# First key quarter turned by TensorE, one MLP copy on VectorE, later side work on ScalarE

## The chip, the cores and the metric

The kernel runs on one core of one Trainium2 chip. The metric is the device time of one launch in microseconds (us), as a median over runs. Five engines work side by side, each through its own list of instructions in order: TensorE (PE, matmuls; PEld is its weight load), VectorE (DVE), ScalarE (ACT), GpSimd (POOL) and SyncE (SP, which mostly issues DMAs). DMA queues move data between HBM and the on-chip SBUF. Matmuls write to PSUM, from which DVE and ACT read.

## The reference

The input x has 2048 tokens of 512 values. After a LayerNorm, two branches start from the same xn:

```python
xn = _layernorm(x, axis=-1)
s = attention(xn, k_cache, v_cache, wq, wo)   # 32 heads of 128, 2048 keys, all softmaxed
h = gelu(layernorm(xn) @ w1)                  # 512 -> 512
hs = shift_by_quarters(h) @ w2                # token shifts +1, -1, +2, -2
x1 = xn + hs
g = silu(x1 + gelu(layernorm(x1) @ w3) @ w4)  # 512 -> 1792 -> 512
return x + s * g
```

All tensors are bf16; the keys and values are given per head as 2048 x 128.

## The kernel before, in words

The attention is cut into 128 **units**: 8 groups of 4 heads, 4 blocks of 512 queries in each group, 4 heads in each block. A unit has 8 **slots** (`n` counts slots over all units, `p` is the slot in the unit). In each slot PE makes two 128x512 score matmuls (`ps_s<-qT,kT`), ACT takes the exponential of both (`s_slot`, L222), and PE multiplies an older slot's result with V (`ps_o<-pT,vb`, `pv_slot`), 4 to 12 slots behind. There are two score buffers in PSUM and two buffers for `ps_o`. DVE adds the exponentials of a unit (`add_first` L228, `add_next` L233), folds the sum (`fold`, L237 and L238), and at the end multiplies `ps_o` with the reciprocal sum (`norm`, L305), which frees the `ps_o` buffer. For the first four and the last two units the row sums are made by PE (`sums`, `ps_sum<-ones_t,acc`); for all others the folded sum is turned by a DMA and reduced by DVE (`turned(u)` says which).

The order is written out by hand: one loop over `n` emits, for each slot, the score matmuls, the V matmuls, then the side work of that slot. Side work is the Q projection, the Wo products (`wo_todo` holds those that are due, as pairs of slots 4 and 5) and the MLP. The MLP is a queue of chunks, some matmuls of which are taken in slots 2, 3, 6 and 7. Stage 1 (w1) has 16 chunks, one for each tile of 128 tokens; its results carry a scale per token. The result of a chunk in `ps_m` is copied to `pre` (L591) by ACT. Two chunks make a pair, and a gelu follows: `square` (ACT, L550) twice, `poly` (DVE, L554), `tanh` (ACT, L559) twice, `last` (DVE, L562).

Which slot ACT's squares and tanhs get is decided by a running **debt**. Each slot adds `EXP_OVER` (0.2) and subtracts the side matmuls that PE had in it; each side operation of ACT adds `SMALL` (2.4). A waiting operation in `act_late` goes out when the debt plus its own cost is covered by the side matmuls that `ahead` sees in the next two slots. `at(n, fn)` puts a function off to slot `n`, `soft(n)` moves it to slot 3, 5 or 7.

The start, before the loop: x tiles are loaded (SP and ACT queues), weights by POOL's queue, and the keys of head 0 in four quarters by transposing DMAs on SP (L173; `KSPLIT` is 4). Meanwhile PE runs 48 small matmuls on the identity (`warm_up`, L125). `first_stats` (L418) makes the LayerNorm of the first four tiles; tile 0 is normalised by ACT (L442). `first_tokens` turns the four tiles by matmuls with the identity, copies them to `xnT` (L492, L490), makes the first queries, copies them to `qT` (L505, L503), and takes the first scores in four groups of quarter and half (`s_half`, exponential L513). The first group reads key quarter 0, the second quarter 1.

All matmuls have the line L125, that of the helper `mm`. A helper `pin` keeps each instruction in the order in which it is written.

Of the kernel before, what the change touches and what calls it, by code (L numbers as in the profile page):

```python
# [8 lines left out]
ACT = mybir.ActivationFunctionType  # L9
# [8 lines left out]
def kernel(  # L18
# [15 lines left out]
    nc = tc.nc  # L34
# [133 lines left out]
    def load_k(h, pieces):  # L168
        w = Sk // KSPLIT
        for i in pieces:  # L170
            if i == 0:
                kTs[h] = kp.tile([P, Sk], BF16, name="kT")
            pin(nc.sync.dma_start(  # L173
                out=kTs[h][:, i * w:(i + 1) * w],
                in_=A_k_cache[0, h, i * w:(i + 1) * w, :], transpose=True))

    def load_v(h, halves, eng=nc.sync):
        v = A_v_cache[0, h].rearrange("(i p j) d -> p i j d", p=P, j=KJ)
# [86 lines left out]
    def turned(u):  # L265
        return T0 <= u < T1
# [148 lines left out]
        pin(nc.vector.bn_aggr(out=mv1[t][:], in_=bn[:]))  # L415
        rsqrt(rs1[t][:], mv1[t][:, 1:2])

    def first_stats():  # L418
        junk = gtp.tile([P, D], BF16, tag="pre", name="pre")
        pin(nc.scalar.activation(  # L420
            out=junk[:], in_=ln[3][:], func=ACT.Identity, scale=1.0 / D, accum_out=mvA[:, 3, 0:1]))
        pin(nc.scalar.activation(
            out=junk[:], in_=ln[3][:], func=ACT.Square, scale=-1.0, bias=mvA[:, 3, 0:1],
            accum_out=mvA[:, 3, 1:2]))
        xn0 = ph1.tile([P, D], BF16, tag="xn", bufs=5, name="xn")
        nb = smp.tile([P, 1], FP32, tag="nm", name="nb")

        def power(t):
            pin(nc.gpsimd.tensor_tensor(
                out=rsA[:, t:t + 1], in0=mvA[:, t, 1:2], in1=nhalf[:, 0:1], op=ALU.pow))  # L430

        for t in range(3):
            pin(nc.vector.bn_stats(out=bnA[:, t, 0:2, :], in_=ln[t][:]))
            pin(nc.vector.bn_aggr(out=mvA[:, t, :], in_=bnA[:, t, :, :]))
            power(t)
            if t == 1:
                pin(nc.vector.tensor_scalar(
                    out=nb[:], in0=mvA[:, 0, 0:1], scalar1=rsA[:, 0:1], scalar2=-1.0, op0=ALU.mult, op1=ALU.mult))
                pin(nc.vector.tensor_scalar(
                    out=mvA[:, 3, 1:2], in0=mvA[:, 3, 1:2], scalar1=1.0 / D, scalar2=EPS, op0=ALU.mult, op1=ALU.add))  # L440
                power(3)
        pin(nc.scalar.activation(  # L442
            out=xn0[:], in_=ln.pop(0)[:], func=ACT.Identity, scale=rsA[:, 0:1], bias=nb[:]))
        xn1 = ln1_norm(1)
        xn3 = ln1_norm(3)
        return xn0, xn1, ln1_norm(2), xn3
# [6 lines left out]
    def ln1_norm(t):  # L453
        xin = ln.pop(t)
        xn = ph1.tile([P, D], BF16, tag="xn", bufs=5, name="xn")
        norm1(t, xn[:], xin[:])
        return xn
# [9 lines left out]
    def warm_up(n):  # L467
        wt = psS.tile([P, 2, 512], FP32, name="ps_s")
        for _ in range(n):
            mm(wt[:, 0, 0:P], ident[:], ident[:], True, True)  # L470
# [111 lines left out]
    def gelu_chunk(lhs, rhs, j, scale, dest):  # L582
        def run(i, n):
            if i == 0:
                mlp["ps"] = psX.tile([P, 512], FP32, tag="xm", name="ps_m")
            mm(mlp["ps"][:], lhs(i), rhs(i), i == 0, i == DC - 1)
            if i == DC - 1:
                if j == 0:
                    mlp["pre"] = gtp.tile([P, 2, 512], BF16, name="pre")
                pre = mlp["pre"]  # L590
                pin(nc.scalar.activation(out=pre[:, j, :], in_=mlp["ps"][:], func=ACT.Identity,  # L591
                                         **({} if scale is None else dict(scale=scale))))
                debt[0] += SMALL
                if j == 1:
                    gelu_pair(pre, dest(), n)
        run.size = DC
        return run
# [200 lines left out]
    pin(nc.scalar.activation(out=act1[:], in_=nhalf[:, 0:1], func=ACT.Identity))  # L798
    for h in range(HG - 1):
        load_w(h, nc.gpsimd)  # L800
    load_k(0, range(KSPLIT))
    load_v(0, (0, 1))
    for i in range(2):
        load_k(1, (2 * i, 2 * i + 1))
        load_v(1, (i,))
    warm_up(WARM)
    xns_0 = first_stats()
    load_w(HG - 1, nc.gpsimd)
    for t in range(4, 6):
        ln1_load(t, nc.gpsimd)  # L810
# [52 lines left out]
    def normed(u):  # L863
        norm(u)
        gg, qq, hh = units[u]
        if hh == HG - 1 and (gg, qq) in deferred:
            at((u + 4) * SPU + 4, lambda: pin(nc.sync.dma_start(out=o_d[(gg, qq)][:], in_=oTs[(gg, qq)][:])))
        elif hh == HG - 1:
            wo_todo.extend((gg, 4 * qq + ts) for ts in range(4))
            if gg == NG - 1:  # L870
                fin_load(4 * qq)

    for n in range(NS):
# [24 lines left out]
            turned_sums(u - 2)  # L898
        if p == 0 and u >= 1:
            add_next(u - 1, 3)  # L900
            if not turned(u - 1):
                fold(u - 1)
        if p == (1 if mlp.get("stage") == 2 or u >= QUIET else 2) and HG < u < NU - 2:
            q_copy(u + 2)
# [3 lines left out]
            acc_turn(u - 1)  # L908
        if p == 1 and u > LATE:
            normed(u - 3)  # L910
        if p == (3 if u >= LATE else 2) and u >= 2 and turned(u - 2):
            bcast(u - 2)
        if n in norms:
# [44 lines left out]
            fn()  # L958
        x = mm_count[0] - mm_before - 4
        debt[0] = max(0.0, debt[0] + EXP_OVER - x) if n >= HALF else 0.0  # L960
        if act_late and debt[0] + SMALL <= ahead(n + 1) + ahead(n + 2):
            act_late.popleft()(n)
            debt[0] += SMALL
        if p == SPU - 1 and u >= 2 and turned(u - 2) and (u < LATE or u == NU - 1):
# [96 lines left out]
```

## Time and profile before

| What | us |
|---|---|
| Median of three runs | 1247.88 |
| Lowest and highest run | 1246.97, 1249.35 |
| The profiled execution | 1246.4 |
| Its span, first to last instruction | 1244.6 |
| PE busy | 1232.4 |
| ACT busy | 1129.0 |
| DVE busy | 1116.5 |
| ACT exponentials (L222), 1020 of them | 1017.7 |
| Span up to the first matmul on keys | 9.01 |

The profile gives for every engine its busy time and, by groups of instructions, the idle time ahead of them and what ended it. Matmuls overlap in the array, so one can last longer than the distance from its start to the next one's. A row of the timeline has the start, the time to the end of the last of the merged instructions, the engine, the line, what is written and read, and in brackets the idle time before it and what ended it. The granted TensorE clock is at full speed in nearly every slice of the span.

### The profile page before, as it was taken

Reading aid. Unit: us, or ns where it says so; the run is one execution under the profiler, and the core shown is the slowest. Engines: PE = TensorE matmul, PEld = TensorE weight load, DVE = VectorE, ACT = ScalarE, POOL = GpSimd, SP = SyncE. Lnnn points to the kernel's source line nnn. Section 1 sums busy time; section 2 is a strip of 40 time slices with the busy share of each in tenths; the row PEclk is TensorE's granted clock in tenths of the full one; section 3 lists DMA queues with packets and bytes.
Section 4 is the critical chain, followed back from the end, with each engine's and each line's share of the span. In section 5 each row is a group of like instructions: output and inputs, shape, how many; then the busy total and the mean of one; then the engine's idle time right before and its main releaser. Section 6 shows DMA issues by size and latency. Waiting matters only on the chain.

```text
span 1244.6 us, 16527 instructions
## 1 busy us (share of the span) xinstructions
PE 1232.4 (99%) x5702; PEld 597.3 (48%) x5816; DVE 1116.5 (90%) x1520; ACT 1129.0 (91%) x1285; POOL 172.2 (14%) x299
## 2 busy tenths in 40 slices
PE   9999999999999999999999999999999999999998
PEld 5444444444444444444444444444444444444444
DVE  7999999999899988899988889999888999888998
ACT  8999998888999888899998889998888999998992
POOL 5563003432111000000100000010000000000110
PEclk9999999999999999999999999999999999999999
DMA  9665573665634455234474235734446233563563
GB/s 202 124 118 101 101 141 77 129 126 123 145 65 112 100 102 120 55 89 75 109 148 90 68 77 111 132 76 82 86 101 124 56 89 65 127 140 76 105 149 108
DMA packets 248788, 131.42 MB, mean 106 GB/s; under 512 B 200000, under 2 KB 225472, under 8 KB 248704
## 3 DMA queue, kind: packets, MB, share of 16 engines
q1 hardware_dynamic: 239296, 104.46, 40.8%
q0 software_dynamic: 8832, 25.44, 9.3%
q8 instruction: 45, 0.74, 0.3%
q10 hardware_dynamic: 576, 0.46, 0.1%
q14 instruction: 39, 0.32, 0.1%
HBM read 83.62 MB, written 8.13 MB: 74 GB/s over the span
## 4 chain that ended last, share of the span: by engine, by line
PE 93%; DVE 3%; ACT 1%; DMA 1%; issue 1%; SPq 0%; DVEq 0%; ACTq 0%
PE ps_o L125 34%; PE ps_s L125 33%; PE ps_m L125 9%; PE ps_q L125 8%; PE ps_wo L125 8%; DVE acc L233 1%; ACT pT L222 1%; DMA kT<-in_A_k_cache_dram 1%; DVE oT L305 0%; DVE acc L228 0%; DMA rb<-dr 0%; DVE acc L237 0%; DVE sm L276 0%; DVE sq L554 0%; DVE s_acc L391 0%
## 5 line engine op out<-in xcount | busy, mean ns | idle before, releaser
L222 ACT ACTIVATE pT<-ps_s 128x1024 bf16<-128x1024 f32 x1020 | 1017.7, 1029 | 89.2 <-PE ps_s L125 72.9
L125 PE MATMUL ps_o<-pT,vb 128*128 128x512 bf16 x2027 | 602.9, 379 | 3.8 <-DVE oT L305 0.2
L125 PE MATMUL ps_s<-qT,kT 128*128 128x512 bf16 (+1 forms) x1992 | 595.3, 378 | 2.2 <-DMA kT<-in_A_k_cache_dram 0.7
L125 PEld LDWEIGHTS <-kT 128*128 128x128 bf16 x2056 | 232.4, 113 | 227.2 <-issue 2.4
L233 DVE TENSOR_TENSOR acc<-acc,pT 128x2048 bf16<-128x2048 bf16 x256 | 310.5, 1213 | 15.6 <-ACT pT L222 14.7
L125 PEld LDWEIGHTS <-vb 128*128 128x128 bf16 x2048 | 200.2, 98 | 225.8 <-issue 0.5
L228 DVE TENSOR_TENSOR acc<-pT 128x2048 bf16<-128x2048 bf16 x128 | 156.2, 1220 | 32.2 <-ACT pT L222 31.8
L125 PE MATMUL ps_q<-xnT,wq_h 128*128 128x512 bf16 (+1 forms) x517 | 151.3, 374 | 0.5
L125 PE MATMUL ps_wo<-wo_h,oT 128*128 128x512 bf16 (+1 forms) x453 | 133.8, 377 | 0.2
L305 DVE TENSOR_TENSOR oT<-ps_o,rb 128x512 bf16<-128x512 f32 x122 | 130.8, 1072 | 2.1 <-DMA rb<-dr 2.0
L391 DVE TENSOR_TENSOR s_acc<-ps_wo,s_acc 128x512 f32<-128x512 f32 x96 | 66.0, 687 | 41.2 <-PE ps_wo L125 40.5
L237 DVE TENSOR_TENSOR acc<-acc 128x1024 bf16<-128x1024 bf16 x128 | 87.4, 683 | 0.3
L276 DVE TENSOR_REDUCE sm<-accT 128x4 f32<-128x512 bf16 x122 | 82.8, 678 | 1.5 <-DMA accT<-acc 1.4
L125 PEld LDWEIGHTS <-wq_h 128*128 128x128 bf16 x524 | 50.7, 98 | 59.5 <-issue 0.8
L208 DVE CAST qT<-ps_q 128x512 bf16<-128x512 f32 x109 | 75.0, 688 | 3.1 <-PE ps_q L125 2.8
L125 PE MATMUL ps_m<-xn2T,w_sb 128*128 128x512 bf16 x218 | 75.3, 379 | 0.1
L125 PE MATMUL ps_m<-w_sb,h2T 128*128 128x512 bf16 x218 | 75.3, 379 | 0.1
L723 POOL DMA_DIRECT2D w_sb<-in_B_w_dram x28 | 21.1, 755 | 370.2 <-PE ps_m L125 328.4
L125 PEld LDWEIGHTS <-oT 128*128 128x128 bf16 x468 | 45.7, 98 | 54.5 <-DVE oT L312 0.5
L751 POOL DMA_DIRECT2D g_d<-xr x16 | 8.8, 548 | 438.3 <-DVE xr L749 438.3
L238 DVE TENSOR_TENSOR acc<-acc 128x512 bf16<-128x512 bf16 x128 | 54.4, 425 | 4.4
L554 DVE SCALAR_TENSOR_TENSOR sq<-sq,pre 128x1024 bf16<-128x1024 bf16 x36 | 44.0, 1222 | 4.6 <-ACT sq L550 4.5
(102 smaller groups left out, 633.5 us busy)
## 6 DMA issues: line engine op xcount, KB each, us to landing
rb<-dr SPq DMA_DIRECT2D x127, 256.0 KB, 3.8
vb<-in_A_v_cache_dram SPq DMA_DIRECT2D x62, 256.0 KB, 3.8
w_sb<-in_B_w_dram POOLq DMA_DIRECT2D x28, 256.0 KB, 4.6
wo_h<-in_A_wo_dram SPq DMA_DIRECT2D x32, 128.0 KB, 3.8
wq_h<-in_A_wq_dram SPq DMA_DIRECT2D x28, 128.0 KB, 3.5
kT<-in_A_k_cache_dram SPq DMA_TRANSPOSE x128, 3.8
dr<-rc SPq DMA_DIRECT2D x128, 2.0 KB, 2.4
xr<-in_A_x_dram POOLq DMA_DIRECT2D x16, 128.0 KB, 3.3
```

Source lines behind the costliest of these rows:

```text
L125: pin(nc.tensor.matmul(out=out, lhsT=lhsT, rhs=rhs, start=start, stop=stop))
L208: pin(nc.vector.tensor_copy(out=qT[:], in_=st[u].pop("psq")[:]))
L222: pin(nc.scalar.activation(out=s["pT"][-1][:, jj:jj + 2, :], in_=sps[:], func=ACT.Exp, scale=SCALE))
L228: pin(nc.vector.tensor_tensor(out=s["acc"][:], in0=s["pT"][0][:], in1=s["pT"][1][:], op=ALU.add))
L233: pin(nc.vector.tensor_tensor(out=a[:], in0=a[:], in1=st[u]["pT"][i][:], op=ALU.add))
L237: pin(nc.vector.tensor_tensor(out=a[:, 0:2, :], in0=a[:, 0:2, :], in1=a[:, 2:4, :], op=ALU.add))
L238: pin(nc.vector.tensor_tensor(out=a[:, 0, :], in0=a[:, 0, :], in1=a[:, 1, :], op=ALU.add))
L276: pin(nc.vector.tensor_reduce(out=sm[:], in_=s.pop("at")[:], axis=mybir.AxisListType.X, op=ALU.add))
L305: pin(nc.vector.tensor_tensor(out=oTs[(g, qt)][:, hh, :].rearrange(f, j=4), in0=s["o"].rearrange(f, j=4), in1=s["rb"].rearrange("x (p j) - ...
L391: pin(nc.vector.tensor_tensor(out=sa, in0=ps[:], in1=sa, op=ALU.add))
L554: pin(nc.vector.scalar_tensor_tensor(out=sq[:].rearrange(f2), in0=sq[:].rearrange(f2), scalar=1.0, in1=pre[:].rearrange(f2), op0=ALU.add, ...
L723: pin(nc.gpsimd.dma_start(out=w[:], in_=w3_v[:, :, fc * P:(fc + 2) * P]))
```

## The change

Four edits go together:

1. The first quarter of head 0's keys is loaded by a plain DMA to a tile `kn` (each partition holds four whole keys), on SP at the place of the first transposing load. Four of the 48 warm-up matmuls become matmuls of `kn` with the identity; four warm-ups follow them. ACT copies the result from PSUM to `kT`, right after it has normalised tile 0 and ahead of the first copy to `xnT`.
2. A stage-1 MLP result whose last matmul lies in slot 3 of a unit is copied to `pre` by DVE, unless a Wo pair is due.
3. `act_late` operations need a margin of 0.4 (2 x `EXP_OVER`) more than before.
4. In units after `LATE` (20) whose predecessor is not turned, the fold of the predecessor stands after the `norm` of slot 1, not in slot 0. This is the case for the last unit alone.

```diff
+    def first_keys():
+        kTs[0] = kp.tile([P, Sk], BF16, name="kT")
+        kn = gtp.tile([P, KJ, Dh], BF16, tag="pre", name="kn")
+        pin(nc.sync.dma_start(
+            out=kn[:], in_=A_k_cache[0, 0, 0:Sk // KSPLIT, :].rearrange("(p j) d -> p j d", j=KJ)))
+        return kn
+
+    def first_keys_turn(kn):
+        tp = psX.tile([P, KJ, P], FP32, tag="xm", name="ps_k")
+        for j in range(KJ):
+            mm(tp[:, j, :], kn[:, j, :], ident[:], True, True)
+        return tp
+
+    def first_keys_back(tp):
+        pin(nc.scalar.activation(
+            out=kTs[0][:, 0:Sk // KSPLIT].rearrange("d (p j) -> d j p", j=KJ), in_=tp[:], func=ACT.Identity))
...
         pin(nc.scalar.activation(
             out=xn0[:], in_=ln.pop(0)[:], func=ACT.Identity, scale=rsA[:, 0:1], bias=nb[:]))
+        behind()
         xn1 = ln1_norm(1)
...
-                pin(nc.scalar.activation(out=pre[:, j, :], in_=mlp["ps"][:], func=ACT.Identity,
-                                         **({} if scale is None else dict(scale=scale))))
-                debt[0] += SMALL
+                if scale is not None and n % SPU == 3 and not wo_todo:
+                    pin(nc.vector.tensor_scalar(
+                        out=pre[:, j, :], in0=mlp["ps"][:], scalar1=scale, scalar2=None, op0=ALU.mult))
+                else:
+                    pin(nc.scalar.activation(out=pre[:, j, :], in_=mlp["ps"][:], func=ACT.Identity,
+                                             **({} if scale is None else dict(scale=scale))))
+                    debt[0] += SMALL
...
-    load_k(0, range(KSPLIT))
+    kn_0 = first_keys()
+    load_k(0, range(1, KSPLIT))
     load_v(0, (0, 1))
...
-    warm_up(WARM)
-    xns_0 = first_stats()
+    warm_up(WARM - 8)
+    tp_0 = first_keys_turn(kn_0)
+    warm_up(4)
+    xns_0 = first_stats(lambda: first_keys_back(tp_0))
...
             add_next(u - 1, 3)
-            if not turned(u - 1):
+            if not turned(u - 1) and u <= LATE:
                 fold(u - 1)
...
         if p == 1 and u > LATE:
             normed(u - 3)
+            if not turned(u - 1):
+                fold(u - 1)
...
-        if act_late and debt[0] + SMALL <= ahead(n + 1) + ahead(n + 2):
+        if act_late and debt[0] + SMALL + 2 * EXP_OVER <= ahead(n + 1) + ahead(n + 2):
             act_late.popleft()(n)
             debt[0] += SMALL
```

More of the change, by code (lines that the diff above doesn't have):

```diff
@@ L170, in load_k @@
         for i in pieces:
-            if i == 0:
+            if h not in kTs:
                 kTs[h] = kp.tile([P, Sk], BF16, name="kT")
@@ L416, in ln1_stats, with first_stats @@
         rsqrt(rs1[t][:], mv1[t][:, 1:2])
-    def first_stats():
+    def first_stats(behind):
         junk = gtp.tile([P, D], BF16, tag="pre", name="pre")
```

## The prediction, as it stood before the result

> **What bounds the kernel now.** I read the page's busy times first, then the waits of PE (TensorE), then the chain of waits in time order.
>
> ```profile
> span 1244.6 us, 16527 instructions
> ...
> PE 1232.4 (99%) x5702; PEld 597.3 (48%) x5816; DVE 1116.5 (90%) x1520; ACT 1129.0 (91%) x1285; POOL 172.2 (14%) x299
> ```
>
> ```profile
> PE ps_s L125 <- DMA kT<-in_A_k_cache_dram: 0.7, 2, 0.5
> PE ps_o L125 <- DVE oT L305: 0.2, 1, 0.2
> ```
>
> ```profile
> 2.92 7.28 DMA kT<-in_A_k_cache_dram
> ...
> 13.50 0.43 PE ps_o L125 x2
> ```
>
> PE is busy for 99% of the span. In the second fence (who waited, for what, us, times, longest) it waits 0.7 us for keys and 0.2 us for an oT. The chain charges 0.43 us for two 512-column matmuls, so 0.216 us each is the pace when nothing holds PE; a matmul's own duration, 0.38 us, is longer because they overlap. The rows hide short stalls for that reason, and I look for starts that lie further apart than 0.216 us. The order of the matmuls is the same in both programs after the start, so the change can win only such stalls. It can lose whatever it makes PE wait. About 1 to 2 us is the whole prize; 0.2% of the time, 2.5 us, is about what a measurement of this kernel can tell from no change.
>
> **Part 1: the first key quarter.** Five answers of the timeline (start, us, engine, line) and two of the DMA view (last number: us from issue to landing):
>
> ```profile
> 5.18 0.81 ACT L442 ACTIVATE xn<-xin,nb,rsA 128x512 bf16<-128x512 bf16 x1
> 6.48 1.08 ACT L492 ACTIVATE xnT<-ps_o 128x512 bf16<-128x512 f32 x2 [0.49 <-PE ps_o L125]
> 7.46 0.60 ACT L492 ACTIVATE xnT<-ps_s 128x512 bf16<-128x512 f32 x1
> 8.04 0.38 ACT L505 ACTIVATE qT<-ps_q 128x256 bf16<-128x256 f32 x1
> ```
>
> ```profile
> 5.85 0.28 PE L125 MATMUL ps_s<-ident 128*128 128x128 bf16 x2
> 6.05 0.23 PE L125 MATMUL ps_o<-ident,xn 128*128 128x128 bf16 x1
> ```
>
> ```profile
> 9.01 0.63 PE L125 MATMUL ps_s<-qT,kT 128*128 128x256 bf16 x4 [0.52 <-DMA kT<-in_A_k_cache_dram]
> 9.47 0.60 PE L125 MATMUL ps_q<-xnT,wq_h 128*128 128x128 bf16 x5
> 10.25 0.30 PE L125 MATMUL ps_s<-qT,kT 128*128 128x256 bf16 x1 [0.18 <-DMA kT<-in_A_k_cache_dram]
> ```
>
> ```profile
> 0.73 0.87 SPq L408 DMA_DIRECT2D xin<-in_A_x_dram  x2
> 1.65 1.23 SPq L173 DMA_TRANSPOSE kT<-in_A_k_cache_dram  x1
> ```
>
> ```profile
> 10.91 2.85 ACT L513 ACTIVATE pT<-ps_s 128x1024 bf16<-128x1024 f32 x3 [0.22 <-PE ps_s L125]
> ```
>
> ```profile
> xin<-in_A_x_dram SPq DMA_DIRECT2D x2, 128.0 KB, 2.7
> ```
>
> ```profile
> kT<-in_A_k_cache_dram SPq DMA_TRANSPOSE x1, 7.3
> ```
>
> Removed is a transposing load that was issued at 1.65 us and took 7.3 us to land (8.96), with PE idle 0.52 us for it before 9.01. Added are a plain load, four matmuls in the place of four warm-ups (48 as before), and one ScalarE copy.
>
> *When kn lands.* Issue is at 1.65 us. The nearest row is xin: the same size, row length and queue, 2.7 us, so about 4.4 us. That is the early end. The late end is the transposing load in the same place, 8.96 us. I take 5.2 us, nearer to xin, with an allowance for the wq_h loads of the POOL queue that are then in flight. *When PE needs it.* Two starts share the row at 5.85: (0.28 - 0.22) puts the last warm-up at 5.91 us, 0.055 us after the one before. The first key matmul stands eight from the end, so 5.91 - 7 x 0.055 = 5.53 us. At 5.2 us it waits for nothing.
>
> The Trainium skill, page "DMA: Bandwidth & Descriptors", section "Queues, rings and completion order", says that each DMA engine takes turns between queues, a packet at a time. That speaks against the change: kn would alternate with POOL's weight loads. Had it to take turns like the quarter it replaces, it would land at the late end; had it one turn, at the early end. The trace has both queues open at once but cannot split the two.
>
> *The ScalarE copy.* It has the form of L492: two of them take 1.08 us, so 0.54 us. It stands behind xn (ends 5.99) where ScalarE was idle for 0.49 us, so the first xnT copy slips by about 0.1 us and the row after it too, up to qT, which ends at 8.42 + 0.1. Everything on PE between them waits for those copies anyway.
>
> *Then.* From 5.99 to 6.05 the hand-over to PE took 0.06 us. The first scores start at 8.42 + 0.1 + 0.06 = 8.58 instead of 9.01. Between the first and second group lie 10.25 - 9.01 less 0.18 of waiting, 1.06 us (1.12 us if the whole pace is counted, one record being absent). So the second group starts at 9.64 to 9.70 instead of 10.25, if quarter 1 is there. It is now issued one plain issue (0.87 / 2 = 0.43 us) behind 1.65, at 2.1 instead of 2.92. With 7.3 us to land it is there at 9.4; with the landing of before, at 10.21 (2.92 + 7.28 in the chain). I take 9.4, as the quarter ahead of it is lighter in the same ring. From 10.91 on ScalarE runs its three exponentials without idle time, so it starts 0.55 us earlier as well, and both engines that could hold this stretch are shifted together. I book **-0.5 us**, between -0.6 and, should kn land at 8.96, 8.96 - 5.53 + 0.1 - 0.6 = +2.9 us (the 0.6 is the wait that goes). All other SP issues of the start move forward by 1.23 - 0.43 = 0.8 us; no row has PE waiting for them.
>
> **Part 2: one MLP copy on VectorE.** The instruction lists show what the condition leaves: only one of the 16 copies with a scale moves, that of token tile 5. Five answers of the timeline:
>
> ```profile
> 90.51 0.69 ACT L591 ACTIVATE pre<-ps_m,mv 128x512 bf16<-128x512 f32 x1
> 91.10 1.02 ACT L222 ACTIVATE pT<-ps_s 128x1024 bf16<-128x1024 f32 x1
> ```
>
> ```profile
> 91.55 0.59 PE L125 MATMUL ps_o<-pT,vb 128*128 128x512 bf16 x2
> 92.17 0.38 PE L125 MATMUL ps_s<-qT,kT 128*128 128x512 bf16 x1
> ```
>
> ```profile
> 93.06 1.23 DVE L233 TENSOR_TENSOR acc<-acc,pT 128x2048 bf16<-128x2048 bf16 x1 [0.88 <-ACT pT L222]
> ```
>
> ```profile
> 89.31 0.68 DVE L208 CAST qT<-ps_q 128x512 bf16<-128x512 f32 x1
> ```
>
> The copy holds ScalarE from 90.51 to 91.10, so the exponential that frees a score buffer is late: two ps_o from 91.55 should end their turn at 91.98, the scores start at 92.17. That stall of 0.19 us goes, since the exponential can start 0.59 us sooner. On VectorE the copy costs what a cast of this shape out of PSUM costs, 0.68 us. Queued behind it are the adds of the unit; the next one but one, at 93.06, was idle for 0.88 us ahead of it and swallows 0.68. If that cover were gone, the adds and the release of pT would be 0.68 us late. I book **-0.19 us**, from -0.25 to +0.2.
>
> **Part 3: square and tanh placed by a stricter rule.** 32 of 144 such ScalarE operations move behind one more exponential, and six of them in the first MLP stage stood right behind another side operation. Three answers of the timeline, first and last of five stalls:
>
> ```profile
> 61.28 0.68 ACT L591 ACTIVATE pre<-ps_m,mvA 128x512 bf16<-128x512 f32 x1
> 61.85 0.63 ACT L550 ACTIVATE sq<-pre 128x512 bf16<-128x512 bf16 x1
> ```
>
> ```profile
> 62.97 0.59 PE L125 MATMUL ps_wo<-wo_h,oT 128*128 128x512 bf16 x2
> 63.45 0.38 PE L125 MATMUL ps_s<-qT,kT 128*128 128x512 bf16 x1
> ```
>
> ```profile
> 154.95 0.59 PE L125 MATMUL ps_q<-xnT,wq_h 128*128 128x512 bf16 x2
> 155.43 0.38 PE L125 MATMUL ps_s<-qT,kT 128*128 128x512 bf16 x1
> ```
>
> Copy and square in a row keep the exponentials away for 0.57 + 0.52 us, and PE's next scores start at 63.45 instead of 62.97 + 0.43 = 63.40: 0.05 us each, five times: **-0.24 us**, from -0.4 (the few 0.04 us stalls of later stages) to +0.2 (VectorE's poly and last steps, of which five slip two slots, make something else late). By the order of the programs the matmuls that read their results stand many slots on.
>
> **Part 4: the fold of the last unit but one.** Two answers of the timeline:
>
> ```profile
> 1215.31 0.69 DVE L237 TENSOR_TENSOR acc<-acc 128x1024 bf16<-128x1024 bf16 x1
> 1216.04 0.43 DVE L238 TENSOR_TENSOR acc<-acc 128x512 bf16<-128x512 bf16 x1
> 1216.38 1.07 DVE L305 TENSOR_TENSOR oT<-ps_o,rb 128x512 bf16<-128x512 f32 x1
> ```
>
> ```profile
> 1216.70 0.59 PE L125 MATMUL ps_s<-qT,kT 128*128 128x512 bf16 x2
> 1217.50 0.59 PE L125 MATMUL ps_o<-pT,vb 128*128 128x512 bf16 x2 [0.21 <-DVE oT L305]
> 1217.93 0.23 PE L125 MATMUL ps_sum<-ones_t,acc 128*128 128x1 bf16 x3
> ```
>
> PE could start ps_o at 1216.70 + 0.43 = 1217.13 and starts at 1217.50, because oT, which frees its buffer, stands behind the fold. With oT first, at 1215.31, it ends at 1216.38, and 0.37 us goes. What is late next is the fold: 1216.38 to 1217.47 (0.69 + 0.43), and the ps_sum that reads it would want to start at 1217.93 - 0.37 = 1217.56, its weights a little sooner. I book **-0.3 us**, from -0.37 to -0.1.
>
> Sum: -0.5 - 0.19 - 0.24 - 0.3 = -1.2 us. The profiled execution took 1246.4 us (span 1244.6 and 1.8 around it), so it would be 1245.2 us. It lies 1.5 us below the median of the three runs, 1247.88 us; on the median the sum gives **1246.7 us**.
>
> **The rivals.**
> *The transfer is hidden anyway* (chance 0.2). Quarter 1 still lands at 10.21 us, being held by the weight loads and not by its place. For it: its 7.3 us are mostly waiting. Against it: less data stands ahead of it. Part 1 is then 0, the sum -0.7: 1247.1 us.
> *The ScalarE stalls come back a few slots on* (0.2). ScalarE is busy 91% of the span and VectorE 90%; a late square or copy only moves. For it: most of the 0.05 us stalls lie in the stretch where both are fullest. Against it: PE has side matmuls there that ScalarE's work can hide under. Parts 2 and 3 give 0: -0.8, 1247.1 us.
> *kn is late* (0.1; ends on the other side). PE stands at the key matmuls and xn's turn, which starts at 6.05 now, waits behind them. Each us after 5.53 costs one us. Parts 2 to 4 give -0.73 and part 1 without a wait -0.5, so it decides from 5.5 + 1.2 = 6.7 us on. At 8.96 us it gives +2.9 - 0.7 = +2.2: 1250.1 us. The Trainium skill, page "TensorE: Matmul & The Clock Gate", section "Part 1: The HAM clock gate", has TensorE at half clock until a window of about 3.4 us was busy; a wait there could leave the clock low for another window, for which no row here has a price. The warm-ups' last spacing, 0.055 us, agrees that the clock was full by 5.85.
> *The change does less than it says* is certain for part 2 (one copy) and is in the sum.
>
> **How the numbers follow.** Forecast 0.45, hidden transfer 0.2, stalls that come back 0.2, kn late 0.1, something unseen 0.05. The likeliest is 1246.7 us. The runs of before lie between 0.9 below and 1.5 above their median, and the terms' own ends make -1.6 to +0.2 without a late kn; together 1244.9 to 1249.0, which takes in the first three cases and the milder half of the late kn. Faster by over 0.2% (below 1245.4) needs the forecast's best ends and a favourable measurement: 0.13. Slower by over 0.2% (above 1250.4) needs kn at its late end and more: 0.07. Within 0.2%: 0.80.
>
> **What would show it.** Right: the first scores at about 8.6 us without a wait for a DMA, the second group near 9.7; at 90 us no gap ahead of the scores; copy and square no longer in a row; at 1217 us ps_o two matmul paces after ps_s. Wrong: PE waiting for kn before 6 us, PE waiting for kT near 10 us, or new starts more than 0.216 us apart near the moved side operations.

## The result and the profile after

| | before | after |
|---|---|---|
| Median of 22 runs, us | 1247.05 | 1249.18 |
| Lowest and highest run, us | 1245.97, 1249.35 | 1247.03, 1250.76 |
| The profiled execution, us | 1246.4 | 1247.84 |

The ratio after to before is 1.0014, with a 95% interval of 1.0008 to 1.0020: the changed kernel is about 1.7 us slower, where 1.2 us faster was forecast. The median lies just above the range. The forecast started from 1247.88 us, the median of three runs, which is 0.8 us above that of 22. Three single executions among all those used below, at clocks of 0.34 to 0.62, took 1.6 to 3 times as long and are left out of every median and ratio.

The page of after, its span and busy times:

```profile
span 1246.1 us, 16531 instructions
...
PE 1232.4 (99%) x5702; PEld 598.2 (48%) x5816; DVE 1116.9 (90%) x1521; ACT 1129.7 (91%) x1285; POOL 172.8 (14%) x299
```

PE's busy time is that of before to the tenth. The 1.5 us of span are waits. PE's waits in after (who waited, for what, us, times, longest):

```profile
PE ps_q L125 <- DVE acc L250: 1.9, 1, 1.9
PE ps_s L125 <- DVE ident L87: 1.4, 1, 1.4
PE ps_q L125 <- ACT xnT L510: 0.4, 1, 0.4
```

The wait for keys is gone and so is the one for oT. (The 1.4 us for `ident` is the start of the warm-ups, ahead of everything here.) New is one wait of 1.9 us at a Q projection, and no step of the prediction spoke of it. To place it I lined the two traces up: the exponentials on ACT come in one order in all kernels, so the start of the same exponential in after, less its start in before, says how late after is at that point. It is 0.25 us late at 10.9 us, 0.25 at 28.6, 2.27 at 32.7, and from there the distance shrinks to 1.47 at the end of the span. So there are three parts to explain: +0.25 at the start, +2.02 near 31 us, and -0.80 over the rest.

**The start.** Timeline of after, ACT and then PE (start, us, engine, line):

```profile
5.39 0.81 ACT L459 ACTIVATE xn<-xin,nb,rsA 128x512 bf16<-128x512 bf16 x1
6.30 1.33 ACT L191 ACTIVATE kT<-ps_k 128x512 bf16<-128x512 f32 x1
7.36 1.17 ACT L510 ACTIVATE xnT<-ps_o 128x512 bf16<-128x512 f32 x2
8.41 0.61 ACT L510 ACTIVATE xnT<-ps_s 128x512 bf16<-128x512 f32 x1
9.00 0.38 ACT L523 ACTIVATE qT<-ps_q 128x256 bf16<-128x256 f32 x1
```

```profile
9.44 0.60 PE L125 MATMUL ps_s<-qT,kT 128*128 128x256 bf16 x4
...
10.53 0.27 PE L125 MATMUL ps_s<-qT,kT 128*128 128x256 bf16 x1
```

The key copy (L191) lasts 1.33 us, where the copies of the same size to `xnT` last 0.61. From the start of xn to the first `xnT` copy it is 7.36 - 5.39 = 1.97 us, where before had 6.48 - 5.18 = 1.30. So the first scores start at 9.44, later than the 9.01 of before, although nobody waits for keys any more.

**The gate near 31 us.** PE in after, then in before, around the new wait:

```profile
30.44 0.59 PE L125 MATMUL ps_o<-pT,vb 128*128 128x512 bf16 x2
32.94 0.59 PE L125 MATMUL ps_q<-xnT,wq_h 128*128 128x512 bf16 x2 [1.90 <-DVE acc L250]
```

```profile
30.19 0.59 PE L125 MATMUL ps_o<-pT,vb 128*128 128x512 bf16 x2
30.66 0.59 PE L125 MATMUL ps_q<-xnT,wq_h 128*128 128x512 bf16 x2
```

These are the first queries of the second block of 512, and the last of the four token tiles that they read is tile 7, which a DMA on SP turns to `xnT`. That DMA in after and in before (last number: us from issue to landing; issued at 25.33 and 26.75):

```profile
xnT<-xn SPq DMA_TRANSPOSE x1, 7.5
```

```profile
xnT<-xn SPq DMA_TRANSPOSE x1, 3.8
```

It lands at 32.85 in after, and the queries start 0.09 us later. The releaser that the row names, an add on DVE, had ended at 32.12; the wait is for the DMA. In before it landed at 30.57, and there too the queries start 0.09 us later, at 30.66, where PE's pace would have had them at 30.19 + 0.43 = 30.62. So the gate held PE in before already, by 0.04 us, and no list of waits shows so little.

**Parts 2 to 4.** PE near 65 and 94 us and at the end, then DVE, all of after:

```profile
65.08 0.59 PE L125 MATMUL ps_wo<-wo_h,oT 128*128 128x512 bf16 x2
65.51 0.38 PE L125 MATMUL ps_s<-qT,kT 128*128 128x512 bf16 x1
...
93.57 0.59 PE L125 MATMUL ps_o<-pT,vb 128*128 128x512 bf16 x2
94.00 0.59 PE L125 MATMUL ps_s<-qT,kT 128*128 128x512 bf16 x2
...
1218.53 0.59 PE L125 MATMUL ps_s<-qT,kT 128*128 128x512 bf16 x2
1218.96 0.59 PE L125 MATMUL ps_o<-pT,vb 128*128 128x512 bf16 x2
```

```profile
92.70 0.74 DVE L610 TENSOR_SCALAR pre<-ps_m,mv 128x512 bf16<-128x512 f32 x1
...
1217.15 1.08 DVE L322 TENSOR_TENSOR oT<-ps_o,rb 128x512 bf16<-128x512 f32 x1
1218.13 0.70 DVE L254 TENSOR_TENSOR acc<-acc 128x1024 bf16<-128x1024 bf16 x1
```

Each of the stalls that parts 2 to 4 aimed at is gone: in all three places two matmuls are followed 0.43 us later by the next ones, the pace of a PE that nothing holds. The matmuls of both programs stand in one order after the start, so each can be set beside itself: after makes up 0.05 us at each of the five places of part 3 (63, 78, 126, 141 and 155 us of before), 0.19 us at that of part 2 and 0.37 us at that of part 4.

### The profile page after: what moved, and what is told of

The parts are those of the page before. It is cut to its first block, busy times and chain, and to the rows that moved or that the text cites. A ratio compares the mean times of both kernels' runs of the same rounds, so it can differ in the third digit from the quotient of the medians.

```text
span 1246.1 us, 16531 instructions
## 1 busy us (share of the span) xinstructions
PE 1232.4 (99%) x5702; PEld 598.2 (48%) x5816; DVE 1116.9 (90%) x1521; ACT 1129.7 (91%) x1285; POOL 172.8 (14%) x299
## 4 chain that ended last, share of the span: by engine, by line
PE 93%; DVE 3%; ACT 2%; issue 1%; DMA 0%; POOL 0%; POOLq 0%
PE ps_o L125 34%; PE ps_s L125 33%; PE ps_m L125 9%; PE ps_q L125 8%; PE ps_wo L125 8%; ACT pT L239 2%; DVE acc L250 1%; DVE acc L254 0%; DVE qT L225 0%; ACT pT L531 0%; DVE bn L431 0%; DVE acc L245 0%; DMA dr<-rc 0%; DVE oT L322 0%; DVE oT L329 0%
## 5 line engine op out<-in xcount | busy, mean ns | idle before, releaser
L408 DVE TENSOR_TENSOR s_acc<-ps_wo,s_acc 128x512 f32<-128x512 f32 x96 | 66.1, 688 | 42.2 <-PE ps_wo L125 41.2
```

The source lines that it names most:

```text
L408: pin(nc.vector.tensor_tensor(out=sa, in0=ps[:], in1=sa, op=ALU.add))
```

## The experiments

My theory after the two traces: parts 2 to 4 do what was forecast, and part 1 loses, through its copy, and through the gate near 31 us. The rivals: kn comes late and its time in after was luck; and the gate has nothing to do with part 1. The first four kernels ran on one chip, the next four on another, e9 to e11 on a third, e12 on a fourth, each beside runs of before.

| Kernel | median, us | ratio to before (95%) | at 10.9 | at 28.6 | at 32.7 | at 71.8 | end of span |
|---|---|---|---|---|---|---|---|
| after | 1249.18 | 1.0014 (1.0008 to 1.0020) | +0.25 | +0.25 | +2.27 | +2.06 | +1.47 |
| e1 part 1 alone | 1249.32 | 1.0017 (1.0008 to 1.0026) | +2.95 | +2.95 | +3.77 | +3.60 | +3.39 |
| e2 parts 2 to 4 alone | 1246.90 | 1.0001 (0.9993 to 1.0010) | -0.43 | -0.43 | +0.48 | +0.26 | -0.44 |
| e3 order changed in PSUM | 1247.74 | 1.0008 (0.9999 to 1.0017) | +2.08 | +2.07 | +2.28 | +2.06 | +1.34 |
| e4 later token loads | 1250.27 | 1.0032 (1.0022 to 1.0043) | +1.35 | +1.35 | +1.31 | +5.36 | +4.61 |
| e5 weights behind kn | 1247.68 | 1.0005 (0.9996 to 1.0014) | +0.24 | +0.24 | +1.23 | +1.02 | +0.10 |
| e6 token loads on SP | 1247.02 | 1.0001 (0.9992 to 1.0010) | +1.39 | +1.38 | +1.35 | +1.13 | +0.34 |
| e7 = e3 + e5 + e6 | 1247.62 | 1.0007 (0.9998 to 1.0016) | +0.24 | +0.24 | +0.21 | +1.05 | -0.04 |
| e8 = e2 + e6 | 1245.51 | 0.9990 (0.9981 to 0.9998) | -0.65 | -0.65 | -0.68 | -0.08 | -0.82 |
| e9 key copy on DVE | 1247.61 | 1.0010 (1.0001 to 1.0019) | -0.37 | -0.37 | +0.95 | +1.43 | +0.34 |
| e10 = e8, earlier Wo loads | 1245.82 | 0.9995 (0.9987 to 1.0004) | -0.58 | -0.58 | -0.61 | +0.14 | +0.96 |
| e11 = before again | 1246.22 (one run) | | -0.43 | -0.43 | +0.17 | +0.01 | -0.18 |
| e12 = before + e6's move | 1246.56 | 0.9999 (0.9990 to 1.0008) | -0.45 | -0.44 | -0.48 | +0.27 | +0.18 |

The last five columns are the lateness described above, in us against the profiled execution of before, at its times. They come from one profiled execution each and tell the mechanism; the ratio tells the size.

**e1_first_quarter_alone**: part 1 stays, the others are undone.

```diff
-                if scale is not None and n % SPU == 3 and not wo_todo:
+                if False:
...
-        if act_late and debt[0] + SMALL + 2 * EXP_OVER <= ahead(n + 1) + ahead(n + 2):
+        if act_late and debt[0] + SMALL <= ahead(n + 1) + ahead(n + 2):
...
-            if not turned(u - 1) and u <= LATE:
+            if not turned(u - 1):
                 fold(u - 1)
...
             normed(u - 3)
-            if not turned(u - 1):
-                fold(u - 1)
```

> Part 1 of the change alone, parts 2 to 4 undone. Theory A (the loss sits in the start: the strided ScalarE copy of the keys, 1.33 us instead of 0.54, and the turned xn tile 7 that now lands late and holds PE for 2 us near 31 us): 2 to 3 us slower than before, and the profile shows PE standing at ps_q near 31 us. Theory B (that stall is an accident of the one profiled execution, and the loss comes from the moved side work of parts 2 and 3): within 0.5 us of before.

Measured: 1.0017, as slow as the whole change. The start is worse than in after. Its load of kn, and what PE did (DMA view, timeline):

```profile
kn<-in_A_k_cache_dram SPq DMA_DIRECT2D x1, 128.0 KB, 5.8
```

```profile
7.45 0.40 PE L125 MATMUL ps_k<-ident,kn 128*128 128x128 bf16 x4 [1.61 <-DMA kn<-in_A_k_cache_dram]
```

In after this load took 3.1 us and landed at 4.79; here it landed at 7.40, and PE stood for 1.61 us. What came next is in the table by stretches (busy us of PE, PEld, DVE, ACT, POOL with counts, then the granted clock, the DMA share and GB/s):

```profile
9.50:10.50 1.00, 0.83 (x9) 0.83 (x9) 0.00 (x0) 1.00 (x3) 0.00 (x0) 0.50 1.11 320
10.50:11.50 1.00, 1.00 (x10) 0.88 (x9) 0.69 (x1) 0.44 (x2) 0.00 (x0) 0.50 1.07 337
11.50:12.50 1.00, 0.95 (x7) 0.66 (x6) 0.00 (x0) 0.03 (x1) 0.00 (x0) 0.50 1.34 322
```

After the wait the clock was 0.50 for some three microseconds, so what PE had to do there took twice as long. Part 1 is the loss (e2, without it, is 2.4 us faster by the median on the same chip), and the late kn is a cause of its own beside the gate.

**e2_without_first_quarter**: parts 2 to 4 stay.

```diff
-    kn_0 = first_keys()
-    load_k(0, range(1, KSPLIT))
+    load_k(0, range(KSPLIT))
...
-    warm_up(WARM - 8)
-    tp_0 = first_keys_turn(kn_0)
-    warm_up(4)
-    xns_0 = first_stats(lambda: first_keys_back(tp_0))
+    warm_up(WARM)
+    xns_0 = first_stats(lambda: None)
```

> Parts 2 to 4 alone, the first key quarter loaded as before. Theory A: 0.8 us faster than before (0.5 to 1.0), no stall at ps_q near 31 us. Theory B: 1.5 to 2 us slower than before.

Measured: 1.0001. The loss goes with part 1, but the interval is too wide to show a gain of 0.7 us. The trace has it: from 32.7 us to the end it gains 0.92 us. Its first quarter landed at 7.39 us and nobody waited for it; and by 32.7 us it had lost 0.91 us without part 1, 0.36 at a row sum at 28.7 us and 0.56 at the gate near 31 us.

**e3_strided_in_psum**: the four matmuls write PSUM in the order of the keys, so that ACT copies in order.

```diff
-        tp = psX.tile([P, KJ, P], FP32, tag="xm", name="ps_k")
+        tp = psX.tile([P, P, KJ], FP32, tag="xm", name="ps_k")
         for j in range(KJ):
-            mm(tp[:, j, :], kn[:, j, :], ident[:], True, True)
+            mm(tp.rearrange("d p j -> d j p")[:, j, :], kn[:, j, :], ident[:], True, True)
...
-            out=kTs[0][:, 0:Sk // KSPLIT].rearrange("d (p j) -> d j p", j=KJ), in_=tp[:], func=ACT.Identity))
+            out=kTs[0][:, 0:Sk // KSPLIT].rearrange("d (p j) -> d p j", j=KJ), in_=tp[:], func=ACT.Identity))
```

> The changed kernel, but the four key matmuls write PSUM with the stride and the ScalarE copy writes SBUF in order. Theory A: the copy takes about 0.6 us instead of 1.33 and the first scores start about 0.7 us sooner, near 8.7 us; the stall near 31 us stays or grows, because the late landing does not depend on the copy: total 0 to 0.7 us faster than the changed kernel, 1 to 2 us slower than before. Theory C (the late start itself shifts the work against the transfers, so that the copy is the one cause): both go, and it is 0.5 to 1 us faster than before.

Measured: 1.0008. PE and ACT in its timeline:

```profile
7.29 0.61 PE L125 MATMUL ps_k<-ident,kn 128*128 128x128 bf16 x4 [1.98 <-DMA kn<-in_A_k_cache_dram]
```

```profile
7.94 0.60 ACT L191 ACTIVATE kT<-ps_k 128x512 bf16<-128x512 f32 x1 [1.93 <-PE ps_k L125]
```

The copy in order takes 0.60 us, so it is the stride of the write that costs the other 0.7. In this execution the wait for kn hid that gain, and the clock was 0.50 from 8 to 11 us.

**e4_later_token_loads**: after, with POOL's loads of the token tiles 10 to 12 issued later, out of the time when tile 7 is turned.

```diff
-            at({11: 24, 12: 25}.get(t, max(stats - 8, 2)), lambda t=t: ln1_load(t, nc.gpsimd))
+            at(27 if t in (10, 11, 12) else max(stats - 8, 2), lambda t=t: ln1_load(t, nc.gpsimd))
```

> The changed kernel with three of the five token loads that the POOL queue issues from 24 to 27 us (tiles 10 to 12) put behind the statistics of tile 8, so that they start near 39 us. Theory A (the turn of xn tile 7 collides with them): it lands before 31.5 us instead of 32.85, the stall at ps_q shrinks from 2.07 us to under 0.7, and the kernel is 1 to 2 us faster than the changed one, within 0.7 us of before on either side. Theory D (the turn is late by what stands ahead of it in SP's own queue, and the token loads do not matter): no difference from the changed kernel, 1.7 us slower than before.

Measured: 1.0032, the slowest of all. Its waits on PE:

```profile
PE ps_sum L125 <- DVE qT L225: 2.8, 1, 2.8
PE ps_k L125 <- DMA kn<-in_A_k_cache_dram: 1.8, 1, 1.8
```

The gate near 31 us is open (tile 7 landed at 30.37, 4.0 us after its issue; the lateness does not grow from 28.6 to 32.7). But the loads that moved were issued at 41.2 to 42.4 us and landed at 47.6 to 49.7, too late for DVE's statistics of those tiles; DVE stood for 2.96 us and PE behind it for 2.8 us near 45 us. Behind that wait the clock was 0.50 from 48.66 to 52.07 us, which cost another 1.3 us. The move cured one gate and closed the next.

The clock can be read further here. In all 14 traces it changes only in steps of 3.41 us, counted from its first rise (between 4.06 and 7.20 us, where the starts of PE's small matmuls go from 0.107 us apart to 0.056). The step ahead of e1's drop, then e4's first step and the one ahead of its drop (columns as in e1's table):

```profile
5.94:9.35 3.41, 1.29 (x20) 1.17 (x21) 1.24 (x5) 1.62 (x3) 3.31 (x6) 1.00 1.14 130
```

```profile
4.29:7.70 3.41, 1.59 (x28) 1.42 (x26) 2.74 (x9) 1.87 (x4) 3.16 (x6) 1.00 1.03 158
45.25:48.66 3.41, 1.04 (x5) 0.43 (x4) 1.03 (x3) 1.78 (x2) 0.45 (x2) 1.00 1.34 306
```

Every step at full clock in which PE was busy for 1.43 us (e3) or less was followed by one at 0.50, eight in all, five of them at the program's end; none with 1.57 us (after, at the gate near 31 us) or more was. So it is not the longest wait that counts here, but how much of the waiting falls into one step.

**e5_weights_behind_keys**: after, with the three Wq loads on SP, behind kn, not on POOL's queue beside it.

```diff
-    for h in range(HG - 1):
-        load_w(h, nc.gpsimd)
     kn_0 = first_keys()
-    load_k(0, range(1, KSPLIT))
+    for h in range(HG - 1):
+        load_w(h)
+        load_k(0, (h + 1,))
```

> The changed kernel with the three first Wq loads moved from the POOL queue to SP, behind kn, each ahead of one key quarter. Theory E (kn lands near 7 us in most executions because its last packets wait on engines that are busy with POOL's Wq loads): kn lands before 5 us, PE does not wait for it, and with the strided copy left the first scores start 0.2 to 0.5 us later than before. The gate near 31 us (turned xn tile 7) is left, so the end is between 0.5 us faster and 1.5 us slower than before. Theory F (kn waits for the x loads or for the start of its queue): it lands near 7 us again, 1.5 to 2.5 us slower than before.

Measured: 1.0005. Two rows of its DMA view:

```profile
kn<-in_A_k_cache_dram SPq DMA_DIRECT2D x1, 128.0 KB, 3.8
...
xnT<-xn SPq DMA_TRANSPOSE x1, 5.1
```

kn landed at 5.43 and PE did not wait. Still the kernel is 0.24 us late at 10.9 us: with kn in time, what is left of part 1 at the start is the copy. From the start of xn on ACT to the first scores it is 9.43 - 5.19 = 4.24 us. At the gate tile 7 landed at 31.64 and PE lost 1 us.

**e6_token_loads_on_sp**: after, with the loads of the token tiles 10 to 12 on SP's queue, where the turn of tile 7 is too.

```diff
-            at({11: 24, 12: 25}.get(t, max(stats - 8, 2)), lambda t=t: ln1_load(t, nc.gpsimd))
+            at({10: 24, 11: 24, 12: 25}.get(t, max(stats - 8, 2)),
+               lambda t=t: ln1_load(t, nc.sync if t in (10, 11, 12) else nc.gpsimd))
```

> The changed kernel with the loads of token tiles 10 to 12 moved from the POOL queue to the end of SP's queue at that point (near 36 us). Theory E (the turn of xn tile 7 is a second gate, late by POOL's token loads): it lands before 31 us, PE stands at ps_q near 31 us for under 0.3 us, and nothing stands at 45 us as it did with the same loads near 41 us. What is left is the late kn and the strided copy, so 0.5 to 2 us slower than before. Theory G (the turn is late by SP's own queue): stall as in the changed kernel.

Measured: 1.0001. The turn of tile 7:

```profile
xnT<-xn SPq DMA_TRANSPOSE x1, 3.8
```

It landed at 30.20, and the gate is open with nothing closed later. kn took 5.3 us here and PE waited 1.8 us for it, with the clock at full speed after the wait.

**e7_all_three**: the edits of e3, e5 and e6 together, after at its best.

> All three repairs: Wq loads behind kn on SP, the stride in PSUM, token loads 10 to 12 on SP. Theory E: first scores 0.3 to 0.5 us earlier than before, no gate near 31 us, parts 2 to 4 give 0.8 us: 1.0 to 1.5 us faster than before. If a gate is left that I have not seen, 0 to 0.8 us faster.

Measured: 1.0007, no better than e6. Its start, PE and ACT:

```profile
5.63 1.06 PE L125 MATMUL ps_k<-ident,kn 128*128 128x128 bf16 x4
```

```profile
6.73 0.60 ACT L191 ACTIVATE kT<-ps_k 128x512 bf16<-128x512 f32 x1 [0.71 <-PE ps_k L125]
```

kn is in time and the copy is short, but the stride went to the matmuls: four of them end after 1.06 us where after's took 0.63, since each starts 0.213 us behind the one before and not 0.107. ACT waits 0.71 us for them. The first scores start at 9.43, as in e5. The gate near 31 us is open, and a third one shows at 54 us, where PE waits 0.9 us for an oT.

**e8_rest_and_tokens_on_sp**: e2 with the move of e6, no part 1.

> Parts 2 to 4 without the plain key load, with token loads 10 to 12 on SP. Theory E: no gate near 31 us, start as before: 0.8 to 1.2 us faster than before, and steadier than parts 2 to 4 alone. The distance to the kernel with all three repairs is what a plain key load is worth at best, about 0.3 us.

Measured: 0.9990 (0.9981 to 0.9998), 1245.51 us. This is the version that beats both kernels, though the interval only just leaves out 1 and it is the best of twelve. Its first scores, the load of its first key quarter, the turn of tile 7, and one of PE's waits:

```profile
8.54 0.60 PE L125 MATMUL ps_s<-qT,kT 128*128 128x256 bf16 x4
```

```profile
kT<-in_A_k_cache_dram SPq DMA_TRANSPOSE x1, 6.2
...
xnT<-xn SPq DMA_TRANSPOSE x1, 2.5
```

```profile
PE ps_wo L125 <- DVE oT L329: 0.6, 1, 0.6
```

The transposing load landed at 7.84 and nobody waited for it. The first scores start at 8.54, the very time that part 1 was forecast to give, with part 1 left out. Of the 0.65 us that this start is ahead, 0.6 are lost again by 71.8 us, most of it at the oT near 54 us.

**e9_key_copy_on_vectore**: part 1 with kn ahead of the weights (e5), the token loads on SP (e6), and the key copy on DVE behind its three normalised tiles. The new edit, without the move of its call:

```diff
-        pin(nc.scalar.activation(
-            out=kTs[0][:, 0:Sk // KSPLIT].rearrange("d (p j) -> d j p", j=KJ), in_=tp[:], func=ACT.Identity))
+        pin(nc.vector.tensor_copy(
+            out=kTs[0][:, 0:Sk // KSPLIT].rearrange("d (p j) -> d j p", j=KJ), in_=tp[:]))
```

> The changed kernel with the Wq loads behind kn on SP, token loads 10 to 12 on SP, and the key copy taken from ScalarE and given to VectorE, behind its three normalised tiles, where it is idle for 1.5 us. Theory H (a plain key load without its costs brings nothing, because the transposing quarter usually lands before the queries are ready, as in the runs without part 1): first scores near 9.1 us minus nothing to gain, that is -0.3 to -0.7 us against the profiled execution of before, the same as with parts 2 to 4 and the token loads alone, and equal to that kernel in time within 0.5 us. Theory A (the load is worth 0.5 us once its costs are gone): 0.4 us or more faster than that kernel.

Measured: 1.0010. The copy, and the first scores:

```profile
7.23 1.29 DVE L191 CAST kT<-ps_k 128x512 bf16<-128x512 f32 x1
```

```profile
8.82 0.60 PE L125 MATMUL ps_s<-qT,kT 128*128 128x256 bf16 x4
```

DVE pays the same for the stride. Off ACT's chain it costs less (8.82 - 5.26 = 3.56 us from the start of xn), but there is no gain over e8 (8.54 - 5.25 = 3.29). Tile 7 came at 31.36 here in spite of the move of e6, and PE lost 1.35 us; e7 has the same loads in the same places, and its tile came at 29.96. So the move of the token loads makes the gate likely to be open, not certain.

**e10_earlier_wo_loads**: e8 with the four Wo loads issued at slot 23.

```diff
-        at(31 + h, lambda h=h: load_wo(h))
+        at(23, lambda h=h: load_wo(h))
```

> Parts 2 to 4 without the plain key load, token loads 10 to 12 on SP, and the four Wo loads of the first group issued before those, near 36 us, instead of at 45 us. Theory I (a third gate of the same kind stands at 54 us: the reciprocal of unit 3 waits in a full queue behind Wq, xn and Wo transfers, PE 0.8 us): dr and rb land about 0.5 to 1 us sooner, the wait at 54 us shrinks below 0.3 us, and the kernel is 0.3 to 0.8 us faster than without the move, 1.5 to 2 us faster than before. Theory J (rb is late by its own chain from VectorE): no difference from the kernel without the move.

Measured: 0.9995 (0.9987 to 1.0004). Near 54 us PE still lost 0.95 us, so those loads do not make it. In the profiled execution a stall of another kind shows, which may be this execution's own (the timeline of ACT near 102 us):

```profile
101.68 0.69 ACT L613 ACTIVATE pre<-ps_m,mv 128x512 bf16<-128x512 f32 x1 [1.73 <-DVE sq L580]
```

It begins at a transfer: at 95.76 us DVE had waited 1.39 us for rb.

**e11_before_again**: before, profiled once more, to see how steady its own trace is.

> The kernel of before, profiled once more. Theory H (the wait of 0.52 us for the first key quarter belongs to the one execution that the prediction read): the quarter lands somewhere between 7.3 and 9 us, and in most executions PE does not wait for it at all. Theory A (it lands near 9 us in every execution): PE waits 0.4 to 0.6 us for it again.

Its first scores, and the gate:

```profile
8.76 0.60 PE L125 MATMUL ps_s<-qT,kT 128*128 128x256 bf16 x4
...
29.77 0.59 PE L125 MATMUL ps_o<-pT,vb 128*128 128x512 bf16 x2
30.84 0.59 PE L125 MATMUL ps_q<-xnT,wq_h 128*128 128x512 bf16 x2 [0.48 <-issue]
```

There is no wait for keys: the quarter landed at 7.55 us, not at 8.96. And 0.64 us are lost at the gate (30.84 - 29.77 - 0.43), where the first trace of before lost 0.04. Of two executions of the same kernel one waits at the keys and the other at the gate, and they end 0.18 us apart.

**e12_token_loads_alone**: before with the move of e6, to see whether e8's gain is that move.

> The kernel of before with nothing but token loads 10 to 12 moved from the POOL queue to SP. Theory E (the gate near 31 us is what limits the first 36 us of the kernel of before, and parts 2 to 4 are worth 0.8 us of the 1.2 us by which both together win): the turn of tile 7 lands before 30 us, PE stands at ps_q near 31 us for under 0.3 us, the wait for oT near 54 us takes most of it back, and the kernel is 0 to 0.6 us faster than before. Theory K (the moved token loads alone make the win and parts 2 to 4 are worth nothing): 1.0 to 1.5 us faster than before.

Measured: 0.9999 (0.9990 to 1.0008). The turn of tile 7:

```profile
xnT<-xn SPq DMA_TRANSPOSE x1, 2.7
```

It landed at 28.78, the gate is open, and the kernel is no faster: what it has in hand at 32.7 us, 0.48 us, is lost by 71.8, most of it near 54 us, where PE starts 0.91 us behind its pace for want of the oT. Its matmuls at the places of parts 2 and 4, both undone here:

```profile
91.82 0.59 PE L125 MATMUL ps_o<-pT,vb 128*128 128x512 bf16 x2
92.44 0.59 PE L125 MATMUL ps_s<-qT,kT 128*128 128x512 bf16 x2
...
1217.41 0.59 PE L125 MATMUL ps_s<-qT,kT 128*128 128x512 bf16 x2
1217.84 0.59 PE L125 MATMUL ps_o<-pT,vb 128*128 128x512 bf16 x2
```

The stall of part 2 is there (0.62 us between the starts where 0.43 is the pace), and so are the five of part 3. That of part 4 is not, although the fold stands in its old place. At the places of parts 2 and 3 e8 makes up 0.44 us and e12 nothing. By the timing, neither parts 2 to 4 alone (e2, 1.0001) nor the move alone shows a gain, so the times do not say how e8's is shared.

## Why the prediction was wrong, point by point

The step that failed is part 1, booked at -0.5 us. Against the profiled execution of before, the seven kernels with it and ScalarE's copy stand at +0.24 to +2.95 us at 10.9 us, the five without it at -0.43 to -0.65, and e9, with the copy on DVE, at -0.37. Its terms, and the other steps, in turn:

- **Parts 2 to 4: right in the mechanism, and part 4's size was one execution's.** I booked -0.19 - 0.24 - 0.3 = -0.73 us. Matmul for matmul, all ten kernels with these parts lack the stall of 0.19 us and the five of 0.05, and all three traces without them (e1, e11, e12) have them. Part 4's stall was 0.37 us in the trace that I read, 0.18 in e1 and e11 and absent in e12, so it is worth 0 to 0.37 us, and the three parts together 0.4 to 0.8. The cover of the DVE copy (0.74 us, 0.68 forecast) held. By timing alone, e8 at 0.9990 beside e12 at 0.9999 agrees, but their intervals overlap.
- **"When kn lands" (5.2 us): failed.** With POOL's Wq loads beside it, kn landed at 4.79 (after), 7.40 (e1), 7.25 (e3), 6.93 (e4) and 6.97 us (e6); PE waited 1.6 to 2.0 us in four of five. The rival "kn is late", with a chance of 0.1, was the usual case, though below its late end of 8.96. With the Wq loads on the same queue behind it, kn landed at 5.43 (e5), 5.11 (e7) and 5.45 us (e9), and nobody waited. So it is the other queue's traffic that makes it late, when it is late. "When PE needs it" (5.53) came from one execution too: the key matmuls started at 5.63 us in after, e5, e7 and e9, where the starts of PE's matmuls were still 0.107 us apart; in e3, e4 and e6, where they went to 0.056 before 4.7 us, PE stood ready for kn at 5.16 to 5.31, where a landing at 5.43 or 5.45, as in e5 and e9, would have been waited for. The Trainium skill, page "DMA: Bandwidth & Descriptors", section "Queues, rings and completion order", says that engines take turns between queues; I quoted it against the change, allowed 0.8 us for it (5.2 after 4.4 us) and booked no wait. These runs agree with it in direction; how the packets took turns no run here shows.
- **The clock after a wait: left without a price.** Lateness at 10.9 us sorts the kernels with ACT's copy: +0.24 or +0.25 with no wait (after, e5, e7), +1.35 and +1.39 with a wait of 1.8 us and a full clock (e4, e6), +2.95 with a wait of 1.61 us and a clock of 0.50 behind it (e1); e3, whose copy is shorter, had 1.98 us and 0.50 and is at +2.08. So the dropped clock is worth about 1.6 us (e1 against e4). Over all 22 runs, those of after with a mean clock of 1.0 average 1248.3 us (10 runs), with 0.999 1249.2 (6) and with 0.998 1250.1 (6). What decided it was PE's busy time in stretches of 3.41 us (e4 above): 1.29 us (e1) and 1.43 us (e3) were followed by a clock of 0.50, 1.59 (e4) and 1.63 us (e6) were not, though e4 and e6 waited for kn as long. The Trainium skill, page "TensorE: Matmul & The Clock Gate", section "Part 1: The HAM clock gate", speaks of an idle window of about 3.4 us that runs freely. The length and the fall to half agree, but the stretches ahead of these drops were not idle: PE was busy in them for up to 1.43 us.
- **"The ScalarE copy ... 0.54 us": failed.** L492 reads the same shape and writes the same number of elements, but it writes them in order; L191 writes every fourth. It measured 1.33 us (e1 and e5 1.31), in order 0.60 (e3, e7). "The first xnT copy slips by about 0.1 us" was 1.97 - 1.30 = 0.67 us. Against a kernel without part 1 and without a wait for keys, from the start of xn to the first scores: 3.29 (e8 and e12), 3.30 (e10), 3.38 (e11) and 3.51 us (e2), but 4.05 (after) and 4.24 (e5). Part 1 costs 0.5 to 0.95 us there even with kn in time.
- **The 0.52 us to be won: one execution's.** The quarter landed at 8.96 us in the trace that I read, but at 7.4 to 7.8 us in e2, e8 and e11, and none of the five profiled executions with the old load since then (e2, e8, e10, e11, e12) waited for it. In five of six profiled executions there was nothing to win.
- **"Both engines that could hold this stretch are shifted together, I book -0.5": failed.** I took it that what is won at 11 us is there at the end. The queries of the second block wait for a turned tile, and that tile came at 30.57 (before), 30.75 (e11) and 32.85 us (after), whatever the start had won. With POOL's token loads in place PE lost 0.04 (before), 0.56 (e2) and 0.64 us (e11) at the gate without part 1, and 0.23 (e3), 0.86 (e1), 1.03 (e5) and 2.07 us (after) with it. So the gate does not need part 1; whether part 1 makes it worse, seven traces do not show. Where the gate was open and the start not late by more than 0.24 us (e7, e8, e10, e12), the oT near 54 us took 0.6 to 0.84 us. A lead of half a microsecond does not pass these two.
- **"No row has PE waiting" for SP's earlier issues: true of the list of waits, and not enough.** PE lost 0.04 us at the gate in before already. Taking POOL's three token loads out of the way made tile 7 land at 28.5 to 30.4 us in e4, e6, e7, e8, e10 and e12, so their traffic is part of what makes it late; e9 is the exception. From issue to landing the turn took 3.8 to 7.5 us in the seven traces with those loads beside it, 2.5 to 4.0 us in these six, and 4.9 us in e9.
- **The other rivals.** The hidden transfer did not show in after: 10.53 - 9.44 = 1.09 us lie between the first and second scores, the distance without a wait. ScalarE's stalls did not come back at their places in any of the ten kernels, but near 102 us PE lost 0.11 us in e6, 0.18 in e8 and 1.65 in e10, and nothing in the others, and after lost 0.15 us near 1200 us; whether part 3 has a hand in this is not shown.
- **The range.** Its ends do not follow from the figures named for them: the lowest and the highest run of before (1246.97, 1249.35) with -1.6 and +0.2 give 1245.4 to 1249.6 us, which takes in the measured median. The mechanism of part 1 was wrong either way.

What stays open: why tile 7's turn took 7.5 us in after, packet by packet; why e9 lost at the gate; and why e7 is 2.1 us above e8 on the same chip (1247.62 and 1245.51 us) when their profiled executions end only 0.78 us apart. Two of e7's eleven runs had a mean clock of 0.998 and 0.999 and took 1250 us, but the other nine average 1247.3.

## What to carry to other kernels

Ask of every wait that a change is to remove whether a second trace of the same program has it: this one's 0.52 us were gone in the next. Follow what is won to the next place where PE needs a transfer that has its own pace, and look there for arrivals that leave no margin, since a list of waits may not show them. Take the duration of a copy only from a row with the same stride, and that of a load only from a row with the same traffic beside it.

## What the runs showed of the hardware that I had not expected

- A copy of 128x512 from PSUM to bf16 that writes every fourth element takes 1.31 to 1.33 us on ScalarE and 1.29 us on VectorE; in order 0.60 us on ScalarE.
- Matmuls of 128 columns that write every fourth f32 of PSUM start 0.213 us apart (e7), where those in order at the same place start 0.107 us apart (after). Once the pace had risen it was 0.109 us (e3) against 0.056 (e1).
- A wait of PE of 1.6 to 2.0 us can be followed by 3.41 us at a clock of 0.50 (e1, e3), and need not be (e4, e6): in these traces the clock fell when PE had been busy for 1.43 us or less of a stretch of 3.41 us, and stayed when it was 1.57 us or more.
- The same plain load of 128 KB took 3.1 to 5.8 us to land with another queue's loads beside it, and 3.5 to 3.8 us with them behind it on its own.
